# A parameter load moved between the touch read and the gate weights, x8 loaded ahead of the C matrices, and the negated sine table made by VectorE

## The chip, the cores and the metric

The kernel runs on one core of a Trainium2 chip. The metric is the device time of one execution in microseconds (us), a median over several executions. Every execution quoted in this document was with a granted TensorE clock of 1.0, so all may be compared. The span of a profile is 1.7 to 1.8 us shorter than the device time of the same execution. All that is read from a profile comes from one execution of that kernel.

Names in the profile: PE is TensorE (PEld its weight loads), DVE is VectorE, ACT is ScalarE, POOL is GpSimd, SP is SyncE. ACTq and SPq are the parts of ScalarE and SyncE that issue DMAs.

## The reference

```python
xn = layernorm(x)                              # x: [1, 2048, 512] bf16, no scale and shift
# A: a diagonal complex state-space model over 2048 steps
dt      = exp(log_dt)
Lam_bar = exp(dt * (Lambda_re + 1j*Lambda_im))
B_bar   = ((Lam_bar - 1) / Lam)[:, None] * (B_re + 1j*B_im)
Bu      = einsum("bld,pd->blp", xn, B_bar)
h_t     = Lam_bar * h_(t-1) + Bu_t
yA      = 2 * Re(einsum("blp,dp->bld", h, C_re + 1j*C_im)) + xn * Dskip
# B: a gated feed-forward block, F = 1376
yB      = (silu(xn @ w_gate) * (xn @ w_up)) @ w_down
out     = x + yA + yB
```

## The kernel before

The 2048 rows are done in four chunks of 512 rows (four tiles of 128 each). For each chunk the kernel normalises x, multiplies by the gate, up and B matrices, runs the recurrence on VectorE, and multiplies the results by w_down and C into the same accumulators. The complex recurrence is done in a rotating frame: VectorE multiplies by tables `cosT` and `sin2` (sine and negated sine), runs a real scan, and rotates back into `hss`, which is the left operand of the C product. The chunk's last stage on TensorE is `w_down` (line 940) and then `W, hss` (line 953).

Instructions of ScalarE, VectorE and GpSimd are ordered at build time by a list scheduler that works from the estimates `est=`. TensorE's and SyncE's instructions stay in program order. A transposing DMA waits for all DMAs issued earlier, and a plain DMA waits for the last transposing one:

```python
def dma(name, dst, src, writes, nbytes, ..., eng="sp", xpose=False, order=(), **kw):
    after = tuple(after)
    if xpose:
        after = after + tuple(dma_tasks)
        fn = lambda e, ...: e.dma_start_transpose(out=dst, in_=src)
        est, nb = 2000.0, int(nbytes * 1.2)
    else:
        if xp_state[0] is not None:
            after = after + (xp_state[0],)
        ...
```

The loads at the start. `x_load(a)` loads tile a of x and `pload` one 1 KB parameter row. The touch read takes 0.2 KB. `a0`, `a1` and `a2` are the first seven column blocks of the gate weights, by rows: a0 has two of the four row blocks (448 KB), a1 and a2 one each (224 KB).

```python
x_load(0)
x_load(1)
act_q = [dma("ld_touch", tch[0:16], wg_v[0:128:8, :, 0:2], [("tch",)], 16 * 16, eng="act")]
act_q.append(wg_load("a0", 0, 2, eng="act", order=(act_q[-1],)))
x_load(2)
act_q.append(wg_load("a1", 2, 3, eng="act", order=(act_q[-1],)))
wg_load("a2", 3, 4)
x_load(3)
pload("ld_ldt", 2, A_log_dt)
pload("ld_lim", 1, A_Lambda_im)
pload("ld_lre", 0, A_Lambda_re)
dma("ld_wu0", ...); dma("ld_wg1", ...); dma("ld_wu1", ...)     # up weights, the rest of the gate weights
dma("ld_x4", ...)                                              # chunk 1 of x
# ... later, in this order: B_re, B_im (transposing), then
def loads_stage_b2():
    dma("ld_cre", CT[:, 0], A_C_re, ..., xpose=True)
    dma("ld_cim", CT[:, 1], A_C_im, ..., xpose=True)
    dma("ld_x8", x_sb[:, 8:12, :], ...)                        # chunk 2 of x
    dma("ld_wd0", ...); dma("ld_wd1", ...); dma("ld_x12", ...); dma("ld_dsk", ...)
```

ScalarE loads its activation table, with a warm activation, only after its DMA issues. The first tile's `1/sqrt(var + eps)` needs that table: ScalarE takes the root (`sd`), VectorE the reciprocal.

```python
def act_table(func, order):
    g.add("act", lambda e: e.activation(out=sm[:, NSM - 1, 0:1], in_=epst[:], func=func, bias=epst[:, 0:1]), ...)
act_table(AF.Sqrt, (act_q[-1],))
# ...
hold["sd%d" % a] = g.add("act", lambda e: e.activation(out=sd0[:, a:a + 1], in_=mv[:, a, 1:2], func=AF.Sqrt, bias=epst[:, 0:1]), ...)
last = g.add("dve", lambda e, a=a: e.reciprocal(out=rstd[:, a:a + 1], in_=sd0[:, a:a + 1]), ...)
```

## Time and profile before

| | before |
|---|---|
| median of 3 runs (lowest to highest) | 180.06 us (180.05 to 180.52) |
| span of the profiled execution (it took 179.85 us) | 178.1 us |
| TensorE busy | 174.4 us, 98% |
| VectorE busy | 162.3 us, 91% |
| ScalarE busy | 88.8 us, 50% |

The first part of the profile page of the kernel before gives busy us, share of the span and instructions of each engine:

```profile
PE 174.4 (98%) x929; PEld 84.1 (47%) x937; DVE 162.3 (91%) x281; ACT 88.8 (50%) x114; POOL 10.3 (6%) x21
```

The chain that ended last is followed back from the last instruction to whatever released it. Here it is for the kernel before (columns: start us, us, what):

```profile
0.79 2.25 DMA x_sb<-in_A_x_dram
...
4.01 0.30 ACT sd L521
...
7.01 0.28 PE pb L568 x2
7.30 0.78 PE pb L783 x14
...
13.68 11.22 PE pb L742 x52
...
175.79 0.29 DVE x_sb L958
```

The chain leaves DMA, VectorE and ScalarE at 7.01 us. After that it is TensorE alone up to 175.79. So a change can shorten the time only in the first 7 us, or by removing TensorE work.

Three lines of VectorE's timeline of the kernel before. The bracket is the idle time ahead of the instruction and what ended it:

```profile
31.79 1.23 DVE L888 TENSOR_TENSOR rot<-u_sb,cosT 128x2048 bf16<-128x2048 bf16 x1 [2.85 <-ACT cosT L703]
...
40.28 2.47 DVE L479 BATCH_NORM_STATS2 st<-x_sb 128x6 f32<-128x512 bf16 x4 [0.76 <-DMA x_sb<-in_A_x_dram]
...
166.01 2.34 DVE L888 TENSOR_TENSOR hss<-rot 128x2048 bf16<-128x2048 bf16 x2
```

And TensorE's timeline of the kernel before, where it takes up the last chunk's `hss`:

```profile
159.07 9.74 PE L940 MATMUL pb<-wd,hT 128*128 128x512 bf16 x65
168.65 7.11 PE L953 MATMUL pb<-W,hss 128*128 128x512 bf16 x47
```

VectorE waits 2.85 us for the cosine table and 0.76 us for x8. Those are the waits that the change goes after. The last `hss` is ready at 166.01 + 2.34 = 168.35 and TensorE takes it at 168.65. I call this difference, 0.3 us, VectorE's **lead** at the last chunk. It is small: VectorE is nearly a second bound.

ScalarE's timeline of the kernel before, from the gate issues (a0 and a1 in one line) to the first `sd`:

```profile
1.23 0.97 ACTq L400 DMA_DIRECT2D wg<-in_B_w_gate_dram  x2
2.23 1.28 ACT L463 ACT_TABLE_LOAD   x1 [2.23 <-issue]
...
4.01 0.29 ACT L521 ACTIVATE sd<-mv,epst 128x1 f32<-128x1 f32 x1 [0.19 <-DVE mv L519]
```

Left out is the warm activation (3.53 to 3.82). Between it and `sd` there are 0.19 us of idle time: this is all the slack that ScalarE's queue has ahead of the chain.

### The profile page before, as it was taken

How to read it: one execution, taken by the hardware profiler on the slowest of the kernel's cores; microseconds unless marked ns; L12 is line 12 of the kernel's file. 1: busy time of each engine (PE TensorE's matmuls, PEld its weight loads, DVE VectorE, ACT ScalarE, POOL GpSimd, SP SyncE). 2: the span in 40 equal slices, each digit the busy share in tenths (PEclk: the TensorE clock that was granted, in tenths of full speed). 3: DMA queues.
4: the chain of work that ended last, by engine and by line, in shares of the span. 5: the costliest groups of instructions: out<-in, count | busy, mean ns of one | idle time of the engine just before them, and what ended most of it. 6: DMA issues, size and time to landing. Idle time of an engine off the chain costs nothing.

```text
span 178.1 us, 2421 instructions
## 1 busy us (share of the span) xinstructions
PE 174.4 (98%) x929; PEld 84.1 (47%) x937; DVE 162.3 (91%) x281; ACT 88.8 (50%) x114; POOL 10.3 (6%) x21
## 2 busy tenths in 40 slices
PE   8999999999999999999999999999999999999994
PEld 2794444444444444444444444444444444444743
DVE  2958984889799999989999999999999999999983
ACT  4469999999799948016565651000965620000000
POOL 3023300002200000050000000000000000000000
PEclk9999999999999999999999999999999999999999
DMA  5995593669260000001330000001100000000123
GB/s 168 377 328 117 119 118 74 136 179 346 88 121 0 0 0 0 0 31 61 86 64 0 0 0 4 0 0 59 59 0 4 0 0 0 0 0 4 59 77 100
DMA packets 22978, 12.37 MB, mean 69 GB/s; under 512 B 15192, under 2 KB 22968, under 8 KB 22968
## 3 DMA queue, kind: packets, MB, share of 16 engines
q1 hardware_dynamic: 22472, 11.54, 24.9%
q10 hardware_dynamic: 496, 0.69, 1.1%
q8 instruction: 7, 0.11, 0.3%
q14 instruction: 3, 0.02, 0.0%
HBM read 6.46 MB, written 2.10 MB: 48 GB/s over the span
## 4 chain that ended last, share of the span: by engine, by line
PE 95%; DVE 2%; DMA 1%; issue 0%; ACT 0%
PE pb L742 36%; PE pb L940 21%; PE pb L857 16%; PE pb L953 15%; PE pb L783 3%; PE pb L820 2%; DMA x_sb<-in_A_x_dram 1%; PE pb L830 1%; PE pb L568 1%; DVE xn_sb L514 1%; DVE st L527 0%; DVE st L509 0%; ACT sd L521 0%; DVE mv L519 0%; DVE rstd L530 0%
## 5 line engine op out<-in xcount | busy, mean ns | idle before, releaser
L897 DVE TENSOR_TENSOR_SCAN rot<-sm,car,rot 128x512 bf16<-128x512 f32 x32 | 38.9, 1266 | 0.1
L940 PE MATMUL pb<-wd,hT 128*128 128x512 bf16 (+3 forms) x194 | 38.1, 355 | 0.2
L742 PE MATMUL pb<-xnT,wu 128*128 128x512 bf16 x160 | 37.3, 379 | 0.0
L742 PE MATMUL pb<-xnT,wg 128*128 128x512 bf16 x132 | 31.3, 379 | 0.0
L953 PE MATMUL pb<-W,hss 128*128 128x512 bf16 (+2 forms) x140 | 28.1, 355 | 0.2
L857 PE MATMUL pb<-xnT,BT 128*128 128x512 bf16 x128 | 28.1, 379 | 0.0
L940 PEld LDWEIGHTS pb<-wd,hT 128*128 128x128 bf16 (+1 forms) x198 | 18.5, 98 | 19.9
L742 PEld LDWEIGHTS pb<-xnT,wu 128*128 128x128 bf16 x160 | 15.6, 98 | 18.9 <-issue 0.2
L754 ACT ACTIVATE sg<-pb 128x1024 bf16<-128x1024 f32 x20 | 20.2, 1025 | 8.3 <-PE pb L742 7.2
L810 ACT ACTIVATE uf<-pb 128x1024 bf16<-128x1024 f32 x20 | 20.6, 1029 | 6.8 <-PE pb L742 6.7
L953 PEld LDWEIGHTS pb<-W,hss 128*128 128x128 bf16 x144 | 13.4, 98 | 14.3
L742 PEld LDWEIGHTS pb<-xnT,wg 128*128 128x128 bf16 x132 | 12.7, 98 | 15.7 <-issue 0.8
L857 PEld LDWEIGHTS pb<-xnT,BT 128*128 128x128 bf16 x128 | 12.5, 98 | 15.1
L864 ACT ACTIVATE u_sb<-pb 128x1024 bf16<-128x1024 f32 x16 | 16.4, 1027 | 4.6 <-PE pb L857 4.2
L812 DVE TENSOR_TENSOR hT<-sg,uf 128x1024 bf16<-128x1024 bf16 x20 | 13.5, 682 | 0.8 <-ACT uf L810 0.6
L888 DVE TENSOR_TENSOR rot<-u_sb,cosT 128x2048 bf16<-128x2048 bf16 x8 | 9.7, 1218 | 2.9 <-ACT cosT L703 2.9
L958 DVE TENSOR_TENSOR x_sb<-pb,x_sb 128x512 bf16<-128x512 f32 (+2 forms) x18 | 10.8, 622 | 1.2 <-PE pb L953 1.2
L839 ACT ACTIVATE sg<-pb 96x1024 bf16<-96x1024 f32 x2 | 2.0, 1021 | 17.3 <-PE pb L820 17.3
L503 ACT ACTIVATE xn_sb<-x_sb,nmr,rstd 128x512 bf16<-128x512 bf16 x8 | 5.9, 803 | 9.6 <-DVE nmr L500 9.6
L888 DVE TENSOR_TENSOR rot<-rot,cosT 128x2048 bf16<-128x2048 bf16 x8 | 9.7, 1215 | 0.1
L888 DVE TENSOR_TENSOR rot<-rot,sin 128x2048 bf16<-128x2048 bf16 x8 | 9.7, 1216 | 0.0
L888 DVE TENSOR_TENSOR rot<-u_sb,sin 128x2048 bf16<-128x2048 bf16 x8 | 9.7, 1216 | 0.0
(78 smaller groups left out, 144.3 us busy)
## 6 DMA issues: line engine op xcount, KB each, us to landing
out_dram<-x_sb SPq DMA_DIRECT2D x15, 128.0 KB, 1.7
x_sb<-in_A_x_dram SPq DMA_DIRECT2D x3, 512.0 KB, 7.6
wd<-in_B_w_down_dram SPq DMA_DIRECT2D x1, 1280.0 KB, 7.1
wu<-in_B_w_up_dram SPq DMA_DIRECT2D x1, 768.0 KB, 5.0
wu<-in_B_w_up_dram SPq DMA_DIRECT2D x1, 608.0 KB, 7.1
x_sb<-in_A_x_dram SPq DMA_DIRECT2D x4, 128.0 KB, 3.3
wg<-in_B_w_gate_dram SPq DMA_DIRECT2D x1, 480.0 KB, 6.0
wg<-in_B_w_gate_dram ACTq DMA_DIRECT2D x1, 448.0 KB, 3.8
```

What stands on the lines that cost most here:

```text
L503: g.add("act", lambda e, a=a: e.activation(out=xn_sb[:, a % NXN, :], in_=x_sb[:, a, :], func=AF.Identity, scale=rstd[:, a:a + 1], bias=nmr ...
L742: inst = e.matmul(pbank[0:fs, bk, :].rearrange("p (j t) -> p j t", j=4), lhsT=w[:, kt, i * 128:i * 128 + fs], rhs=xnT[:, c % 2, :, kt, :], ...
L754: g.add("act", lambda e: e.activation(out=sg[rows, sl, 0:n, :].rearrange("p a t -> p (a t)"), in_=pair_f32(rows, bk, 512 * n), func=AF.Sil ...
L810: g.add("act", lambda e: e.activation(out=uf[rows, ul, 0:n, :].rearrange("p a t -> p (a t)"), in_=pair_f32(rows, bk, 512 * n), func=AF.Ide ...
L812: g.add("dve", lambda e: e.tensor_tensor(out=hT[rows, hb, i0:i0 + n, :], in0=sg[rows, sl, 0:n, :], in1=uf[rows, ul, 0:n, :], op=ALU.mult), ...
L857: inst = e.matmul(pbank[:, bk, :].rearrange("p (j t) -> p j t", j=4), lhsT=BT[:, ri, kt, pt * 128:(pt + 1) * 128], rhs=xnT[:, c % 2, :, kt ...
L864: g.add("act", lambda e: e.activation(out=u_sb[:, us].rearrange("p r t -> p (r t)"), in_=pair_f32(slice(0, 128), b0), func=AF.Identity), r ...
L888: tt = lambda out, a, b, op, r, w, nm: g.add("dve", lambda e: e.tensor_tensor(out=out, in0=a, in1=b, op=op), reads=r, writes=w, name="%s_% ...
L897: g.add("dve", lambda e, A0=A0, A1=A1, k=k, ri=ri, pt=pt: e.tensor_tensor_scan(out=A1[:, k, ri, :], data0=rr[:, pt:pt + 1].to_broadcast([1 ...
L940: inst = e.matmul(pbank[:, bk, 0:nc_], lhsT=hT[0:fs, hb, i, lt * 128:(lt + 1) * 128], rhs=wd[0:fs, i, c0:c0 + nc_], start=(i == 0), stop=F ...
L953: inst = e.matmul(pbank[:, bk, 0:nc_], lhsT=hss[:, hb, pt, ri, lt * 128:(lt + 1) * 128], rhs=W12[:, ri, pt, c0:c0 + nc_], start=False, sto ...
L958: g.add("dve", lambda e, bk=bk, a=a, c0=c0, nc_=nc_: e.tensor_tensor(out=x_sb[:, a, c0:c0 + nc_], in0=pbank[:, bk, 0:nc_], in1=x_sb[:, a, ...
```

## The change

The intent, as the diff shows it: bring the `log_dt` row in earlier by ScalarE's queue, so that SyncE's queue is free sooner. Load x8 before the two C transposes, so that chunk 2's statistics need not wait. Take the second sine of each table block off ScalarE (-sin is -1 times sin, a cheap bf16 multiply on VectorE), which frees the buffer `tz` earlier for the cosine. Give the scheduler more realistic times for GpSimd and transposing DMAs. The warm activation also loses its bias operand, and one buffer (`tch`) moves.

```diff
--- before.py
+++ after.py
@@ -324,12 +324,12 @@
         mv = sb("mv", [128, NT, 2], F32)
         ve = sb("ve", [128, NT], F32)
         rstd = sb("rstd", [128, NT], F32)
+        tch = sb("tch", [16, KT, 2], B16)
         nmr = sb("nmr", [128, NT], F32)
         mhalf = sb("mhalf", [128, NT], F32)
         st0 = sb("st0", [128, 4, 2, 6], F32)
         sd0 = sb("sd0", [128, 4], F32)
         epst = sb("epst", [128, 1], F32)
-        tch = sb("tch", [16, KT, 2], B16)
         praw = sb("praw", [128, 3, PT], B16)
         prow = sb("prow", [12, 128], B16)
         ecst = sb("ecst", [128, PT], F32)
@@ -393,7 +393,7 @@
             if xpose:
                 after = after + tuple(dma_tasks)
                 fn = lambda e, dst=dst, src=src: e.dma_start_transpose(out=dst, in_=src)
-                est, nb = 2000.0, int(nbytes * 1.2)
+                est, nb = 1900.0, int(nbytes * 1.2) + 140000
             else:
                 if xp_state[0] is not None:
                     after = after + (xp_state[0],)
@@ -422,12 +422,12 @@
         x_load(0)
         x_load(1)
         act_q = [dma("ld_touch", tch[0:16], wg_v[0:128:8, :, 0:2], [("tch",)], 16 * 16, eng="act")]
+        act_q.append(pload("ld_ldt", 2, A_log_dt, eng="act", order=(act_q[-1],)))
         act_q.append(wg_load("a0", 0, 2, eng="act", order=(act_q[-1],)))
         x_load(2)
         act_q.append(wg_load("a1", 2, 3, eng="act", order=(act_q[-1],)))
         wg_load("a2", 3, 4)
         x_load(3)
-        pload("ld_ldt", 2, A_log_dt)
         pload("ld_lim", 1, A_Lambda_im)
         pload("ld_lre", 0, A_Lambda_re)
         dma("ld_wu0", wu[:, :, 0:FH0], wu_v[:, :, 0:FH0], [("wu", 0)], 512 * FH0 * 2)
@@ -440,9 +440,9 @@
             dma("ld_bim", BT[:, 1], A_B_im, [("BT", 1, kt) for kt in range(KT)], 512 * 512 * 2, xpose=True)
 
         def loads_stage_b2():
+            dma("ld_x8", x_sb[:, 8:12, :], x_v[:, 8:12, :], [("x", a) for a in range(8, 12)], 4 * TILEB)
             dma("ld_cre", CT[:, 0], A_C_re, [("CT", 0)], 512 * 512 * 2, xpose=True)
             dma("ld_cim", CT[:, 1], A_C_im, [("CT", 1)], 512 * 512 * 2, xpose=True)
-            dma("ld_x8", x_sb[:, 8:12, :], x_v[:, 8:12, :], [("x", a) for a in range(8, 12)], 4 * TILEB)
             dma("ld_wd0", wd[:, 0:FT - 1, :], B_w_down[0:(FT - 1) * 128, :].rearrange("(k p) d -> p k d", p=128), [("wd", 0)], (FT - 1) * 128 * 1024)
             dma("ld_wd1", wd[0:fsz[-1], FT - 1, :], B_w_down[(FT - 1) * 128:Fh, :], [("wd", 1)], fsz[-1] * 1024)
             dma("ld_x12", x_sb[:, 12:16, :], x_v[:, 12:16, :], [("x", a) for a in range(12, 16)], 4 * TILEB)
@@ -460,7 +460,7 @@
         g.add("pool", lambda e: e.memset(car[:, 0], 0.0), writes=[("car", 0, 0), ("car", 0, 1)], name="car0", est=100)
         g.add("pool", lambda e: e.memset(ecst[:], math.e), writes=[("ecst",)], name="ecst", est=100)
         def act_table(func, order):
-            g.add("act", lambda e: e.activation(out=sm[:, NSM - 1, 0:1], in_=epst[:], func=func, bias=epst[:, 0:1]), reads=[("epst",)], writes=[("sm", "_warm")],
+            g.add("act", lambda e: e.activation(out=sm[:, NSM - 1, 0:1], in_=epst[:], func=func), reads=[("epst",)], writes=[("sm", "_warm")],
                   name="act_warm", est=1500, order=order)
 
         act_table(AF.Sqrt, (act_q[-1],))
@@ -485,11 +485,11 @@
 
         def ln_ve(a, n, eng="dve", order=()):
             return g.add(eng, lambda e: e.tensor_scalar(out=ve[:, a:a + n], in0=mv[:, a:a + n, 1], scalar1=EPS, scalar2=None, op0=ALU.add),
-                         reads=[("mv", a + j) for j in range(n)], writes=[("ve", a + j) for j in range(n)], name="ve%d" % a, est=70 if eng == "dve" else 230, order=order)
+                         reads=[("mv", a + j) for j in range(n)], writes=[("ve", a + j) for j in range(n)], name="ve%d" % a, est=70 if eng == "dve" else 600, order=order)
 
         def ln_rstd(a, n):
             return g.add("pool", lambda e: e.tensor_tensor(out=rstd[:, a:a + n], in0=ve[:, a:a + n], in1=mhalf[:, a:a + n], op=ALU.pow),
-                         reads=[("ve", a + j) for j in range(n)] + [("mhalf",)], writes=[("rstd", a + j) for j in range(n)], name="rstd%d" % a, est=370 + 190 * n)
+                         reads=[("ve", a + j) for j in range(n)] + [("mhalf",)], writes=[("rstd", a + j) for j in range(n)], name="rstd%d" % a, est=1000 + 215 * n)
 
         def ln_apply(a, order=()):
             return g.add("dve", lambda e: e.tensor_scalar(out=xn_sb[:, a % NXN, :], in0=x_sb[:, a, :], scalar1=mv[:, a, 0:1], scalar2=rstd[:, a:a + 1],
@@ -694,8 +694,8 @@
                       reads=[("tt1", b), ("tm", b)], writes=[("tz", b)], name="tzs%d" % pt, est=660, prio=_CFG['prio_tab'])
                 g.add("act", lambda e, pt=pt, b=b: e.activation(out=sin2[:, pt, 0, :], in_=tz[:, b, :], func=AF.Sin, scale=-TWO_PI),
                       reads=[("tz", b)], writes=[("sinT", pt, 0)], name="sinT%d" % pt, est=620, prio=_CFG['prio_tab'])
-                g.add("act", lambda e, pt=pt, b=b: e.activation(out=sin2[:, pt, 1, :], in_=tz[:, b, :], func=AF.Sin, scale=TWO_PI),
-                      reads=[("tz", b)], writes=[("sinT", pt, 1)], name="msinT%d" % pt, est=620, prio=_CFG['prio_tab'])
+                g.add("dve", lambda e, pt=pt: e.tensor_scalar(out=sin2[:, pt, 1, :], in0=sin2[:, pt, 0, :], scalar1=-1.0, scalar2=None, op0=ALU.mult),
+                      reads=[("sinT", pt, 0)], writes=[("sinT", pt, 1)], name="msinT%d" % pt, est=200, prio=_CFG['prio_tab'])
                 g.add("dve", lambda e, b=b: e.tensor_scalar(out=tt1[:, b, :], in0=tm[:, b, :], scalar1=0.25, scalar2=MAGIC, op0=ALU.add, op1=ALU.add),
                       reads=[("tm", b)], writes=[("tt1", b)], name="tt1c%d" % pt, est=400, prio=_CFG['prio_tab'])
                 g.add("dve", lambda e, b=b: e.scalar_tensor_tensor(out=tz[:, b, :], in0=tt1[:, b, :], scalar=MAGIC, in1=tm[:, b, :], op0=ALU.subtract, op1=ALU.subtract),
```

## The prediction

> **What bounds it.** TensorE. The page's busy table gives PE 98% of a 178.1 us span (DVE 91%, ACT 50%), clock 1.0 throughout. The chain of waits is DMA, DVE and ACT only up to 7.01 us (x tile 0 lands 3.04, statistics to 3.98, `sd` 4.01-4.30, reciprocal, normalisation, transposes). From there to 175.79 it is TensorE without a gap over 0.05 us; one 0.29 us DVE add and about 2 us of store end it. So a change pays only in the first 7 us or if it makes TensorE wait later. TensorE's own work is unchanged.
>
> **Parameter load on ScalarE's queue.** The DMA issues there took 0.41 to 0.49 us, this load on SyncE's queue 0.37. It moves the two gate loads and what follows them by about 0.4 us. By the timeline the Sqrt table load (2.23, 1.28 us) and its warm activation (to 3.82) leave 0.19 us before `sd` at 4.01; the Trainium skill, "ScalarE: Activation LUTs", section "What ACT_TABLE_LOAD costs", states about 1283 ns per load, and the trace has 1.28 us. With 0.4 us more in front, `sd` starts near 4.2: +0.2 us on the start of the chain. The gate weights issued at 1.23 land about 5.0, would land 5.4, and are used at 6.0: enough slack. SyncE's later loads go 0.4 us earlier; the x4 load's 0.38 us wait shrinks, off the critical path. Dropping the bias operand of the warm activation saves nothing.
>
> **Negated sine by VectorE.** ScalarE loses four activations of 0.62 us (2.5 us). VectorE gains four bf16 128x512 multiplies; the float32 tensor-scalar of that size took 0.42 us and the bf16 one with two pointer scalars 0.35 to 0.41, so I estimate 0.2 to 0.35 each, 0.8 to 1.4 in all. The buffer `tz` becomes free after one sine rather than two, so the cosine comes earlier: VectorE's 2.85 us wait for `cosT` before 31.79 should shrink to about 1.
>
> **x8 ahead of C.** Chunk 2's x was issued at 36.8 and waited for at 40.28 (0.76 us). It will be issued near 28 and the wait goes. The C transposes (28.5 and 32.6, 4.1 us each) land some 4 us later, near 41, still far before their first use at 55.95. The last W ends at 73.1, its first matmul starts at 75.06.
>
> **Scheduling estimates.** More realistic GpSimd times let the static order fill VectorE's waits for `rstd` (0.86 and 0.60 us).
>
> **Critical path.** VectorE is without idle from 79.4 to 173. `hss` of the last chunk is ready at 168.3 and TensorE wants it at 168.65: 0.3 us of slack. VectorE's reclaimed idle (2 to 4 us) should exceed the 0.8 to 1.4 us added, so the slack grows, but nothing on TensorE gets shorter by it. Remaining: +0.2 us at the start, passed through unchanged.
>
> **Prediction.** 180.2 us, range 179.6 to 181.0. Faster by over 2%: 1%; within 2%: 96%; slower by over 2%: 3%.
>
> **What would show it.** PE busy stays near 174 us. Right: Sqrt table load near 2.6, `sd` near 4.2, the chain entering TensorE near 7.2. Sine line 697 gone from ScalarE, four VectorE multiplies of 0.2 to 0.35 us. DVE wait for `cosT` under 1.5 us; no wait for x8. At the last chunk `hss` ready more than 0.3 us ahead of its matmuls. Wrong: new TensorE waits for `hT`, `xnT`, `hss` or W after 14 us, or gate weights that TensorE waits for.
>
> **What would make it wrong.** The new estimates reorder VectorE's and ScalarE's static streams; a bad order could delay `hss` at 168 or a bank release, costing up to some microseconds. Less early gate-weight traffic may let x tiles 0 and 1 land earlier, giving back the 0.2 us or more. The difference is close to the spread of the three runs (180.05 to 180.52).

## The result

| | before | after |
|---|---|---|
| median of 6 runs each (lowest to highest) | 180.09 us (179.93 to 180.52) | 179.98 us (179.95 to 180.71) |
| ratio after / before, 95% interval | | 0.9999 (0.9981 to 1.0018) |
| span of the profiled execution | 178.1 us | 178.4 us |

A ratio here and below is the mean time of one kernel's fast runs over that of the other's fast runs of the same rounds, so it is not quite the ratio of the medians that stand beside it. The time is the same. The profiled execution of the changed kernel took 180.20 us, one of its slower runs; that of the kernel before took 179.85 us. So the two profiles differ by 0.35 us where the medians differ by 0.11 us the other way, and what the profile of the changed kernel shows at the start need not hold for its four executions at 179.95 to 179.99 us. A second set of runs of the changed kernel (e12 below) came out at 1.0020 (1.0008 to 1.0032). The two intervals overlap from 1.0008 to 1.0018, some 0.15 to 0.3 us slower; the first set alone doesn't exclude no difference at all.

The first part of the page of the changed kernel:

```profile
PE 174.6 (98%) x937; PEld 84.0 (47%) x937; DVE 163.1 (91%) x285; ACT 87.1 (49%) x110; POOL 9.0 (5%) x21
```

The work moved as intended. TensorE's did not change (eight more matmul records are records that the first trace had missed). One group of the kernel before, from the groups by line and shape (columns: line, engine, operation, tiles, count, then busy us and mean ns, then idle time before):

```profile
L697 ACT ACTIVATE sin<-scrC 128x512 bf16<-128x512 f32 x4 | 2.5, 623 | 0.0
```

The same line's group in the changed kernel:

```profile
L697 DVE TENSOR_SCALAR sin<-sin 128x512 bf16<-128x512 bf16 x4 | 1.1, 289 | 0.0
```

2.5 us of ScalarE became 1.1 us of VectorE. Without its bias operand the warm activation takes 202 ns in place of 296 (means of the same view). VectorE's timeline of the changed kernel, at the same three places and at x4's statistics:

```profile
14.47 2.47 DVE L479 BATCH_NORM_STATS2 st<-x_sb 128x6 f32<-128x512 bf16 x4 [1.02 <-DMA x_sb<-in_A_x_dram]
...
29.79 1.23 DVE L888 TENSOR_TENSOR rot<-u_sb,cosT 128x2048 bf16<-128x2048 bf16 x1 [0.23 <-ACT u_sb L864]
...
32.50 2.47 DVE L479 BATCH_NORM_STATS2 st<-x_sb 128x6 f32<-128x512 bf16 x4 [0.35 <-DMA x_sb<-in_A_x_dram]
...
163.92 2.36 DVE L888 TENSOR_TENSOR hss<-rot 128x2048 bf16<-128x2048 bf16 x2
```

TensorE's timeline of the changed kernel at the last `hss`:

```profile
168.98 7.11 PE L953 MATMUL pb<-W,hss 128*128 128x512 bf16 x48
```

The 2.85 us wait is gone (the rotation starts 2.0 us earlier), the x8 statistics start 7.8 us earlier, and the last `hss` is ready at 166.28, a lead of 2.7 us in place of 0.3. TensorE does not get to it sooner: in this execution it arrives 0.33 us later than before. VectorE's gain is real and buys nothing, because the end is set by TensorE. Where do the 0.33 us come from? The chain of the changed kernel:

```profile
1.23 0.58 ACTq L400
...
2.27 5.28 DMA wg<-in_B_w_gate_dram
...
7.60 0.95 PE pb L783 x14
...
14.02 11.22 PE pb L742 x52
...
176.13 0.29 DVE x_sb L958
```

The chain no longer enters TensorE through x, its statistics and its normalisation. It goes through ScalarE's queue: the touch read, the parameter load (0.58 us at 1.23), the issue of a0, the issue of a1 (2.27), and a1's landing at 7.55. TensorE's second group of gate matmuls waits for a1 and starts at 7.60. In the kernel before, a1 was issued at 1.72, landed near 5.9, and nothing waited for it. ScalarE's timeline of the changed kernel:

```profile
1.23 0.58 ACTq L400 DMA_DIRECT2D prow<-in_A_log_dt_dram  x1
...
2.79 1.28 ACT L463 ACT_TABLE_LOAD   x1 [2.79 <-issue]
...
4.20 0.28 ACT L521 ACTIVATE sd<-mv,epst 128x1 f32<-128x1 f32 x1
```

So two things in the first 8 us could account for the later start. The table is late and with it `sd` (4.20 against 4.01), as predicted. And the gate weights are late, which was not predicted. They need separate experiments.

### The profile page after: what moved, and what is told of

Read it like the earlier page. It is cut to its first block, busy times and chain, and to the rows that moved or that the text cites. A ratio compares the mean times of both kernels' runs of the same rounds, so it can differ in the third digit from the quotient of the medians.

```text
span 178.4 us, 2429 instructions
## 1 busy us (share of the span) xinstructions
PE 174.6 (98%) x937; PEld 84.0 (47%) x937; DVE 163.1 (91%) x285; ACT 87.1 (49%) x110; POOL 9.0 (5%) x21
## 4 chain that ended last, share of the span: by engine, by line
PE 94%; DMA 3%; ACTq 1%; DVE 0%; issue 0%
PE pb L742 35%; PE pb L940 21%; PE pb L953 16%; PE pb L857 15%; PE pb L783 3%; DMA wg<-in_B_w_gate_dram 3%; PE pb L820 2%; PE pb L830 1%; ACTq L400 1%; PE pb L568 0%; DVE x_sb L958 0%; PE pb L565 0%
## 5 line engine op out<-in xcount | busy, mean ns | idle before, releaser
L940 PE MATMUL pb<-wd,hT 128*128 128x512 bf16 (+3 forms) x198 | 38.8, 355 | 0.0
```

Of the source, the lines that this page charges most:

```text
L940: inst = e.matmul(pbank[:, bk, 0:nc_], lhsT=hT[0:fs, hb, i, lt * 128:(lt + 1) * 128], rhs=wd[0:fs, i, c0:c0 + nc_], start=(i == 0), stop=F ...
```

## The experiments

Questions and theories:

- **The start.** Theory T: the late table and `sd` cost the time. Rival G: the late gate weights do. (N in the expectations: neither shows in the time.) A further rival on why a1 is so late, S: SyncE's queue issues the up weights (wu0) earlier now and they take the bandwidth.
- **The lead.** Theory: the parts other than the load are neutral because TensorE is the bound, and their value is a lead that can be shown by making VectorE do useless work. Rival: the lead is an accident of the profile, and VectorE's work costs the same in both kernels.
- **Each part alone.** Does the load, x8 or the negation do the same alone as within the whole? Theory D for the load: it delays x4, and by the serial chain of DMAs (x4, B, the normalised x, C, x8) also x8, which in the old order makes VectorE late at the end.

All kernels gave correct results. Two runs fell outside everything that was expected beforehand: e1 and e7 cost clearly more than any theory had given. Each ran over 5 rounds beside the kernel before on the same chip; rows with the same time of before (179.83, 179.87, 179.89) shared one chip and its runs. Times are medians.

| run | what | time, us | before, us | ratio (95%) |
|---|---|---|---|---|
| e1 | before + the load moved | 181.33 | 179.83 | 1.0081 (1.0067 to 1.0095) |
| e2 | after, load back on SyncE | 179.97 | 179.83 | 1.0009 (0.9997 to 1.0022) |
| e3 | after + a second small load ahead of the gates | 180.31 | 179.83 | 1.0024 (1.0012 to 1.0037) |
| e4 | after, load behind the gates | 180.03 | 179.83 | 1.0009 (0.9997 to 1.0022) |
| e12 | after, again | 180.13 | 179.87 | 1.0020 (1.0008 to 1.0032) |
| e10 | before + load moved + x8 ahead | 180.29 | 179.87 | 1.0023 (1.0011 to 1.0035) |
| e11 | after, x8 back behind C | 180.16 | 179.87 | 1.0026 (1.0010 to 1.0042) |
| e7 | before + negated sine | 180.40 | 179.87 | 1.0033 (1.0016 to 1.0050) |
| e5 | before + 2.3 us of useless VectorE work | 181.41 | 179.89 | 1.0086 (1.0070 to 1.0101) |
| e6 | after + the same work | 180.19 | 179.89 | 1.0015 (1.0003 to 1.0027) |
| e8 | before + x8 ahead | 179.91 | 179.89 | 0.9999 (0.9987 to 1.0011) |
| e13 | e2 + one activation for 1/sqrt | 179.41 | 179.89 | 0.9972 (0.9960 to 0.9984) |

### The load alone: e1

```diff
 act_q = [dma("ld_touch", ...)]
+act_q.append(pload("ld_ldt", 2, A_log_dt, eng="act", order=(act_q[-1],)))
 act_q.append(wg_load("a0", 0, 2, eng="act", order=(act_q[-1],)))
 ...
-pload("ld_ldt", 2, A_log_dt)
```

> The kernel before with the log_dt load moved between the touch read and the gate loads on ScalarE's queue, nothing else. Theory G (gate loads): the load's issue (0.58 us in the changed kernel) pushes both gate loads back, the third quarter of the gate weights lands near 7.5 us instead of 5.9, and TensorE's second group of gate matmuls starts near 7.6 instead of 7.3: 180.3 to 180.5 us, +0.2 to +0.4 on the kernel before. Theory T (table): the delay is that of the Sqrt table load (2.8 instead of 2.2) and of the first square root (4.3 instead of 4.0), gate weights in time: the same total, but the chain enters TensorE through VectorE's normalisation. Theory N: both are in the noise, within 0.1 us of the kernel before.

It took 181.33 us, 1.5 us more than the kernel before. This is from a move of one 1 KB load. The chain of e1:

```profile
6.22 8.67 DMA x_sb<-in_A_x_dram
...
33.66 4.08 DMA hss<-in_A_C_im_dram
37.75 3.53 DMA x_sb<-in_A_x_dram
41.31 2.47 DVE st L479 x4
...
168.00 2.28 DVE hss L888 x2
```

Read from the top: x4 lands at 14.9, the transposing DMA of the normalised x starts at 23.48, then come the C transposes at 29.56 and 33.66, then x8, whose statistics start at 41.31 (40.28 before). From there the chain is VectorE to the end. `hss` is ready at about 170.3, some 1.9 us later than before, and the lead of 0.3 us does not cover that: 1.9 - 0.3 = 1.6 us, which fits the measured 1.5. Some 1.0 of the 1.9 us came with x8. For the rest, among VectorE's reordered instructions, I have no cause.

VectorE comes last here, but TensorE is late too. TensorE's timeline of e1:

```profile
8.30 0.95 PE L783 MATMUL pb<-xnT,wg 128*128 128x128 bf16 x14 [0.75 <-DMA wg<-in_B_w_gate_dram]
...
160.11 9.74 PE L940 MATMUL pb<-wd,hT 128*128 128x512 bf16 x66
170.32 7.12 PE L953 MATMUL pb<-W,hss 128*128 128x512 bf16 x48 [0.47 <-DVE hss L888]
```

The second gate group waited for a1 until 8.30, and TensorE reaches its last `w_down` matmuls at 160.11, where the kernel before has 159.07: 1.04 us late, with no other wait between. Of the 1.67 us by which the last C product is late (170.32 against 168.65), VectorE adds only the last 0.6. So in this execution there are two late paths side by side, and taking one away leaves the other.

### The load with x8 ahead: e10; x8 alone: e8; x8 put back: e11

e10 is e1 with this, and e8 is the kernel before with it; e11 is the changed kernel with the opposite:

```diff
 def loads_stage_b2():
+    dma("ld_x8", x_sb[:, 8:12, :], ...)
     dma("ld_cre", ..., xpose=True)
     dma("ld_cim", ..., xpose=True)
-    dma("ld_x8", x_sb[:, 8:12, :], ...)
```

> The load move of the first experiment (181.33 us alone) with x8 ahead of the C matrices added, nothing else of the change. Theory D: the 1.5 us come through the DMA chain: x4 lands about 1.2 us later, each of the transposes waits for all loads before it, so x8 behind C lands late and VectorE waits 2.07 us for it, and VectorE has only 0.3 us to lose. With x8 ahead of C the wait goes and the time is 179.9 to 180.4. Rival G (late gate weights alone at the start): x8 doesn't matter and the time stays at 181.0 to 181.5.

> The kernel before with x8 ahead of the C matrices, nothing else. x8 lands near 31 us; its statistics come before the first rotation in VectorE's order. No change in time is expected, 179.7 to 180.1; VectorE waits for x8 (up to 3 us, where it waited for the cosine before) and hss of the last chunk is ready 1.5 to 2.5 us ahead. The negated sine alone cost 0.5 us because two normalisations of chunk 2 stood ahead of a bank release on ScalarE; with x8 early those come before 45 us and no such wait should show.

> The changed kernel with x8 back behind the C matrices, all else of the change kept. If x8's place is what hides the load's cost, VectorE waits about 1 to 2 us for x8 again and the time is 180.5 to 181.3. If the negated sine alone gives enough lead (2 us less waiting for the cosine), the time stays at 179.9 to 180.3, with hss ready 0.5 to 1.5 us before its matmuls instead of 2.7.

x8 ahead took 1.04 us off the load's cost (181.33 to 180.29, on two chips), with lead 2.0 us in e10's profile. That is what theory D asks for. Of these 1.04 us, though, only the 0.6 us that TensorE lost to `hss` in e1's trace are shown to be VectorE's: e10's start is also less late than e1's (dense matmuls at 13.97, against 14.56 in e1 and 13.52 before), which x8, issued near 29 us, can't have done. How much x8's place is worth in an average execution stays open. Alone, x8 ahead changes nothing (0.9999), though it raises the lead from 0.3 to 2.15 us. That is again lead without time, and such a lead would cover a delay of VectorE from any cause, not only a late x8.

e11 did not mirror this. With the negation and the new estimates kept, x8 back behind C cost little: its profile shows a lead of 3.4 us and no wait for x8. Its ratio, 1.0026, is not apart from e12's 1.0020. Its runs scatter (three of 179.97 to 180.02, three of 180.3 to 180.9), and what the slower three lack is not known, as the profiled one was among the fast. So x8 ahead is one way to gain the lead, and the other parts of the change are another.

### The negated sine alone: e7

```diff
-g.add("act", ... activation(out=sin2[:, pt, 1, :], in_=tz[:, b, :], func=AF.Sin, scale=TWO_PI), ...)
+g.add("dve", ... tensor_scalar(out=sin2[:, pt, 1, :], in0=sin2[:, pt, 0, :], scalar1=-1.0, scalar2=None, op0=ALU.mult), ...)
```

> The kernel before with the negated sine by VectorE, nothing else. Both theories: no change in time, 179.7 to 180.0 us, since TensorE is full; VectorE gains four instructions of 0.29 us, its wait of 2.85 us for the cosine falls under 1, and hss of the last chunk is ready 1 to 2.5 us before its matmuls instead of 0.3. If ScalarE's saved 2.5 us were on the critical path, the time would fall by more than 0.3.

It cost 0.3%, about 0.5 us. In the profile the lead is 2.95 us, so VectorE is not the cause. The chain of e7 shows where TensorE waited:

```profile
48.13 1.41 ACT xn_sb L503 x2
49.54 0.92 ACT uf L810
...
50.51 8.81 PE pb L742 x40
```

TensorE stops for 0.46 us until ScalarE has emptied an accumulator bank (`uf`), and ScalarE was late with that because it first did the four normalisations (`xn_sb`) of the next chunk in one block, 46.62 to 49.55. The order is not new: the kernel before has the same block in the same place, but 0.67 us earlier. ScalarE's timeline of the kernel before, then of e7:

```profile
45.95 2.93 ACT L503 ACTIVATE xn_sb<-x_sb,nmr,rstd 128x512 bf16<-128x512 bf16 x4 [1.04 <-DVE nmr L500]
...
46.62 2.93 ACT L503 ACTIVATE xn_sb<-x_sb,nmr,rstd 128x512 bf16<-128x512 bf16 x4 [1.66 <-DVE nmr L500]
```

The block waits for `nmr` of VectorE, and that for `rstd` of GpSimd. GpSimd's timeline of the kernel before, then of e7:

```profile
43.12 0.58 POOL L487 TENSOR_SCALAR ve<-mv 128x4 f32<-128x4 f32 x1 [23.53 <-DVE mv L483]
...
42.93 1.11 POOL L487 TENSOR_SCALAR ve<-mv 128x4 f32<-128x4 f32 x1 [23.29 <-DVE mv L483]
```

In e7 `ve` took twice as long, `rstd` ended later, and `nmr` started at 46.01 (45.67 before). That is half of the 0.67 us; I have no cause for the other half, nor for the longer `ve`, beside which VectorE now runs other instructions (two rotation products from 42.75). In the changed kernel the four normalisations are at 38.29, 40.01 and 45.08 (two), since x8 and its statistics come earlier, and no such wait follows. In e11, with x8 late again, the block is even later (48.21), but stands behind one `uf` more, and TensorE does not wait either. So the negation alone, which takes work off ScalarE, cost time through a late link from VectorE over GpSimd to ScalarE. In the whole change this does not show; which part covers for it was not tested.

### What the lead is worth: e5 and e6

Both compute one product of chunk 3's two halves twice, with the result unchanged:

```diff
-tt(A0, U, Cb, ALU.mult, ru + rdt, [k0], "pin1")
+for _ in range(2 if c == NCH - 1 else 1): tt(A0, U, Cb, ALU.mult, ru + rdt, [k0], "pin1")
```

> The kernel before with 2.3 us of idle work for VectorE in the last chunk: its first product (1.14 us) computed twice for both halves, same result. If VectorE's lead at the last chunk is the 0.3 us that the trace shows, TensorE waits about 2 us for hss there and the time is 181.4 to 182.1 (+1.6 to +2.2). If the lead is not what counts (TensorE alone bounds it), the time stays within 0.3 us of the kernel before.

> The changed kernel with the same 2.3 us of idle work for VectorE. Its lead at the last chunk is 2.7 us, so the work should fit in: 179.9 to 180.4, within 0.3 us of the changed kernel, hss ready 0.2 to 0.6 us before its matmuls. If the larger lead is an accident of the profile, it loses 1 us or more.

The same 2.3 us of VectorE work cost the kernel before 1.5 us, and the changed kernel nothing that shows: ratio 1.0015, beside 1.0020 for the changed kernel without it (e12, on another chip). TensorE's timeline of e5 at the last `hss`:

```profile
169.90 7.12 PE L953 MATMUL pb<-W,hss 128*128 128x512 bf16 x47 [1.06 <-DVE hss L888]
```

TensorE's timeline of e6:

```profile
169.26 7.11 PE L953 MATMUL pb<-W,hss 128*128 128x512 bf16 x47
```

and VectorE's of e6:

```profile
166.48 2.34 DVE L888 TENSOR_TENSOR hss<-rot 128x2048 bf16<-128x2048 bf16 x2
```

In e5 TensorE waits 1.06 us for `hss`, which is ready 1.48 us later than in the kernel before and not 2.3: VectorE was reordered elsewhere (its wait of 0.76 us for x8 is gone in e5), so the cost of 1.5 us stands at the bottom of what was expected (1.6 to 2.2). In e6 `hss` is ready at 168.82 and the lead is still 0.4 us: 2.7 less the added 2.3. So the lead is real and its size is right in the changed kernel: it can take 2.3 us of VectorE work, and nothing in this kernel spends it.

### The start: e2, e4, e3 and e12

e2 is the changed kernel with the load back on SyncE, e4 with the load on ScalarE's queue but behind the gates, e3 with a second load of the same 1 KB (into a tile that nobody reads) ahead of the gates. e12 is the changed kernel itself.

```diff
 # e2, against after
-act_q.append(pload("ld_ldt", 2, A_log_dt, eng="act", order=(act_q[-1],)))
 ...
 x_load(3)
+pload("ld_ldt", 2, A_log_dt)
 # e4, against after: the same line taken out, and
 act_q.append(wg_load("a1", 2, 3, eng="act", order=(act_q[-1],)))
+act_q.append(pload("ld_ldt", 2, A_log_dt, eng="act", order=(act_q[-1],)))
 # e3, against after
 act_q.append(pload("ld_ldt", 2, A_log_dt, eng="act", order=(act_q[-1],)))
+act_q.append(dma("ld_dum", pdum[:], A_log_dt.rearrange("(a p) -> a p", p=128), [("pdum",)], 1024, eng="act", order=(act_q[-1],)))
```

> The changed kernel with the log_dt load back on SyncE's queue, all else kept. If the load costs at the start (G or T), this is 0.2 to 0.4 us faster than the changed kernel's profiled start: second group of gate matmuls at 7.1 to 7.3 us, total 179.7 to 179.9. VectorE's lead at the last chunk stays at 2 to 3 us. If the load is not it (N), the time stays at 179.9 to 180.1 and the second group stays near 7.6.

> The changed kernel with the log_dt load behind the two gate loads on ScalarE's queue instead of ahead of them; every other instruction of every engine in the same order. Gate loads are issued at 1.2 and 1.7 again, the Sqrt table load stays late (2.8). G: the third quarter of the gate weights lands near 6, the second group of gate matmuls starts by 7.3, time 179.7 to 180.0 (0.1 to 0.3 under the changed kernel). T: the first square root stays at 4.2 or later and the start is as late as in the changed kernel, near 7.5; no gain. A third theory (S): the loss is from SyncE's later weight loads starting 0.34 us earlier and taking bandwidth; then the third quarter still lands after 7 us here.

> The changed kernel with one more parameter load of the same size, into a tile nobody reads, ahead of the gate loads on ScalarE's queue: the dose doubled. G: gate loads 0.4 to 0.6 us later again, TensorE waits for gate weights for 0.5 to 1.2 us in the first 9 us, and the time rises by 0.3 to 0.8 us over the changed kernel. T: the square root moves to about 4.7 and the whole start by 0.4 to 0.6 us, with no wait for gate weights. N: no change over 0.15 us.

> The changed kernel itself again, so that it stands on the same chip and in the same rounds as the others. Within 0.3 us of the kernel before (its first ratio was 0.9999), VectorE's hss of the last chunk ready 2 to 3 us before its matmuls. If the load's cost of 1.5 us measured with the load alone were in it too, it would be at 181.3.

e4 is the run that parts the theories: its table is as late as in the changed kernel, wu0 is issued as early (3.84), and only the gates are not held up. The second gate group in TensorE's timeline of e4:

```profile
7.43 0.94 PE L783 MATMUL pb<-xnT,wg 128*128 128x128 bf16 x14
```

It has no wait for a DMA, nor has the group before it. S is refuted: a1 landed near 6.0 (issued at 1.71, 4.3 us to landing), although wu0 was as early as in the changed kernel. But the start is not back where it was. The chain of e4 runs through the late table:

```profile
2.84 1.28 ACT L463
...
4.34 0.19 ACT sd L521
...
13.85 11.22 PE pb L742 x52
```

By their chains the dense 512-column matmuls start at 13.68 in the kernel before, at 13.85 in e4 and at 14.02 in the changed kernel. So in these three executions T and the late gate weights (G) are worth some 0.17 us each. In e12 and e6, two more traces with the changed kernel's start, the dense matmuls begin at 14.06 and 14.29, and in e11, where TensorE did not wait for gate weights, at 13.81, so the gate weights' part runs from nothing to 0.4 us (and more in e1, at 14.56 by the timeline, which has 13.69 for e4). e2, with neither, should be at the start of the kernel before; it is at 13.81, its chain running through warm-up matmuls that took 0.84 us instead of 0.49 in e4. By what had been expected of them, e2's time (179.97) falls to N and e4's second group (7.43) nearer to T than to G.

The times can't part T from G. e4's ratio equals e2's to the last digit, though its `sd` is at 4.24 and e2's at 4.04, and both intervals are 0.12% wide on either side, about 0.2 us. e12 and e3 lie 0.1% above e2 and e4, about 0.2 us, and the intervals overlap. One point fits: the profiled execution of e11, with the load ahead and no wait, has a span of 178.2 us, as have the four quick executions of the changed kernel, while the five profiled ones of after, e12, e3, e6 and e10, all with the wait, have 178.4 to 178.7. The wait may thus come in some executions only; that was not tested. TensorE waits for gate weights in six of the seven traces with the load ahead of them (after, e1, e3, e6, e10, e12; not e11), and in none of the seven others. In e3, e6 and e12 it was the first group that waited (0.35 us in e3), in the others the second.

A second small load did not double the cost: the issue that comes third in the queue took 0.27 us where the second took 0.58.

a1 was 1.65 us later in the changed kernel than before (7.55 against about 5.9), while its issue was 0.55 us later. The transfers themselves slowed. This is no clean split, however: from issue to landing a1 took 4.2 to 5.2 us in the seven traces without the load ahead of it and 4.6 to 6.0 us in the seven with it. The stretch from 3 to 4 us, by windows (columns: stretch, clock of the stretch, then busy us and instructions of PE, PEld, DVE, ACT and POOL, then granted clock, DMA share and GB/s), of the kernel before:

```profile
3.00:4.00 1.00, 1.00 (x4) 0.36 (x3) 0.88 (x2) 0.81 (x2) 0.00 (x0) 1.00 1.01 326
```

of the changed kernel:

```profile
3.00:4.00 1.00, 1.00 (x4) 0.37 (x3) 0.83 (x2) 1.00 (x1) 0.00 (x0) 1.00 0.90 208
```

and of e4:

```profile
3.00:4.00 1.00, 1.00 (x4) 0.36 (x3) 0.87 (x2) 1.00 (x1) 0.00 (x0) 1.00 1.03 347
```

In this stretch the DMA engines moved 149 to 235 GB/s in all seven traces with the load ahead of the gates and 302 to 347 in all seven without it. Their busy share fell much less (0.70 to 0.92 against 0.92 to 1.03), so mostly they moved fewer bytes in the time that they were busy. Why is open: no run took the load's own transfer and its place in the queue apart.

### A version that beats both: e13

If only the first 7 us count, that is the place for a gain. In e2, ScalarE's root and VectorE's reciprocal of the first chunk are replaced by one activation:

```diff
-act_table(AF.Sqrt, (act_q[-1],))
+act_table(AF.Abs_reciprocal_sqrt, (act_q[-1],))
-... activation(out=sd0[:, a:a + 1], in_=mv[:, a, 1:2], func=AF.Sqrt, bias=epst[:, 0:1])
+... activation(out=rstd[:, a:a + 1], in_=mv[:, a, 1:2], func=AF.Abs_reciprocal_sqrt, bias=epst[:, 0:1])
-last = g.add("dve", lambda e, a=a: e.reciprocal(out=rstd[:, a:a + 1], in_=sd0[:, a:a + 1]), ...)
```

> A version that may beat both: the change without its load move, and in the first chunk the square root by ScalarE plus reciprocal by VectorE replaced by one reciprocal square root on ScalarE. The profiles say that only the first 7 us count: the chain there has two such pairs (reciprocal 0.17 us plus two hand-overs each), so TensorE's continuous work should start 0.2 to 0.4 us earlier, near 6.9, unless the gate weights (third quarter landing 5.9 to 6.9, fourth 6.7) hold it. 179.4 to 179.8 us if the chain counts; 179.8 to 180.0 if the gate weights do.

It took 179.41 us, 0.28% less than the kernel before, with the interval clear of 1, and was correct. The chain of e13 (its lines are two fewer than before):

```profile
7.00 0.78 PE pb L781 x14
...
13.24 11.22 PE pb L740 x52
...
175.35 0.29 DVE x_sb L956
```

The second gate group starts at 7.00. The reciprocal (0.17 us, and the hand-over around it) is gone from each of the first tiles, the dense matmuls start 0.44 us earlier in the chain than in the kernel before (13.24 against 13.68), and the last add is 0.44 us earlier too (175.35 against 175.79). The 0.44 us passed through 162 us unchanged, as the predicted +0.2 was to. Two other ways to the same end never ran: a power on VectorE did not compile, and the language refuses the plain `Rsqrt` activation.

Not tried: the new estimates alone, without any other part of the change.

## Why the prediction was right or wrong

The time, 180.2 us predicted and 179.98 measured (180.13 in the second set), and "within 2%" were right. The number says little, though: a guess of no change (180.06) would have been at least as near, and the forecast +0.2 us came out as -0.11 in the first set of medians and +0.26 in the second. The steps:

- **TensorE is the bound, and a gain elsewhere gives nothing.** Right. e8 (lead up by 1.85 us, time unchanged) and e5 with e6 show it.
- **Negation.** Right: 0.289 us each, within 0.2 to 0.35. The wait for `cosT` fell to 0.23 us on another releaser, under the 1.5 given.
- **Lead at the last chunk.** Right in direction: 0.3 to 2.7 us.
- **`sd` near 4.2.** Right (4.20), but as the sum of two errors. The load's issue took 0.58 us, not about 0.4, so the table came at 2.79 rather than 2.6. And "dropping the bias operand of the warm activation saves nothing" was wrong: it saved 94 ns on the way to `sd` (4.20, against 4.29 in e1, which has the same late table and kept the operand). The Trainium skill, "ScalarE: Activation LUTs", section "What ACT_TABLE_LOAD costs", states that each [128,1] pointer operand adds about 93 ns; the trace agrees (296 to 202 ns). I had read that section for the table load and not applied this line.
- **"The gate weights issued at 1.23 ... enough slack."** This step failed. It looked at a0 only, and took the landing to shift by the issue. a1, the next in the queue, landed 1.65 us later, and TensorE waited for it: the very thing that the prediction named as a sign of being wrong. The chain entered TensorE at 7.60 through a DMA, not near 7.2 through VectorE. The start moved by 0.34 us in the profile rather than 0.2. With the gates out of the way (e4) the step through the table is right: 0.17 us. In time the difference is at the edge of what these runs resolve.
- **"The x4 load's 0.38 us wait shrinks."** Wrong: it grew to 1.02 us. x4 was issued at 5.74 rather than 5.81, but took 8.7 us to land rather than 7.9.
- **"x8 ... the wait goes."** Nearly: 0.35 us of 0.76 stayed, 8 us earlier in the program.
- **"SyncE's later loads go 0.4 us earlier."** True of wu0 (3.84 against 4.18), and lost again on the way to x4, as the issue of wu1 took 0.86 us in place of 0.59.
- **Waits for `rstd` (0.86 and 0.60 us).** Right: neither is left in VectorE's timeline of the changed kernel. Whether the new estimates did it was not tested.
- **Not foreseen at all:** that the parts are not neutral alone. The load alone costs 1.5 us and the negation alone 0.5 us. In the whole neither shows. The prediction's list of risks had "a bad order could delay `hss` at 168 or a bank release", and a late `hss` and a late bank release are what happened, in e1 and e7; but in e1 some 1.0 us of it came with x8's landing, and in e7 with a late `nmr`, not with the order of the engine that was late.

The clearest limit of the evidence: effects of 0.2 us at the start are of the size of the scatter between executions. The three short warm-up matmuls ahead of the first gate group took 0.77 us before, 0.49 after, 0.84 in e2 and 0.85 in e1. The Trainium skill, "TensorE: Matmul & The Clock Gate", section "Part 1: The HAM clock gate", puts the change to full speed about 4 us into the activity, give or take 500 ns from run to run. This scatter agrees in kind, while the profile's granted clock reads 1.0 throughout and does not show it.

## What to carry to other kernels

Ask of each saving which wait of the bound engine it ends; time given back to any other engine is lead, and lead can be measured by giving that engine useless work in both kernels. A tiny DMA may not be free in front of a load that the bound engine needs (in the traces with it the dense matmuls started 0.1 to 1.0 us later than in the kernel before): check every later load in that queue, not only the next one, and what the issuing engine itself does next. Test the parts of a compound change alone as well as together, because one part may hide the cost of another; with a static scheduler even taking work off an engine can move other instructions for the worse.

## What the Trainium skill lacked or had wrong

- "ScalarE: Activation LUTs", section "What ACT_TABLE_LOAD costs": 1283 ns for the load is right (1283 ns in every trace). The drain of about 1380 ns that it adds, 2.66 us per switch, does not show: the next activation started 0.02 us after the load's end (3.53 after 2.23 + 1.28; 4.09 after 2.79 + 1.28). At the second load of the kernel before, a real switch behind an activation, it doesn't show either: the activation ends at 10.53, the load starts at 10.56, and the next activation at 11.85.
- The same page, section "What it computes", advises VectorE's reciprocal with a `Sqrt` activation because `Rsqrt` has known accuracy issues. It does not mention `Abs_reciprocal_sqrt`, which here saved 0.44 us of start (e13: 0.9972).
- "DMA: Bandwidth & Descriptors", section "Issuing engines are not separate DMA queues", calls the sequencer's time to initiate a DMA usually small relative to the DMA. No page says how that time spreads on this chip. Here it was 0.25 to 1.27 us: 0.37 for the 1 KB row on SyncE, 0.58 for the same row second on ScalarE's queue, 0.50 to 1.18 for the same up-weight load (wu1) in different kernels.
- No page says what a 1 KB load in front does to the transfers behind it. Here 326 GB/s before became 208 after at 3 to 4 us, and a1 came 1.65 us later for a 0.55 us later issue; over all traces a1 took 4.2 to 5.2 us without the load ahead and 4.6 to 6.0 us with it. The cause is open.
- "TensorE: Matmul & The Clock Gate" describes the varying moment of full speed; no page says that the profile's granted clock leaves it out (1.0 throughout, while the same three matmuls took 0.49 to 0.85 us).
